# Attention of the last two batches run four groups ahead, and seven products for eight in the last four groups of an attention and mixer kernel

## Chip, core and metric

One NeuronCore of a Trainium2 chip. The metric is the device time of one execution in microseconds (us), the median of several runs. All data are float32.

## What is computed

For 8 batches of 576 tokens, 8 heads of width 64: attention inside chunks of 64 tokens, then a mixer over tokens of rank 32 and a two-layer network over channels (512 to 2048 to 512).

```python
scores = scale * np.matmul(q_c, k_c.transpose(0, 1, 2, 4, 3))   # chunks of 64
attn = softmax(scores); out = np.matmul(attn, v_c)
x = out, heads side by side                                     # 8 x 576 x 512
xt = x.transpose(0, 2, 1)
h = xt @ U @ V                                                  # rank 32, over tokens
u = x + h.transpose(0, 2, 1)
ch = np.maximum(u @ w_ch1, 0.0) @ w_ch2                         # 512 -> 2048 -> 512
return u + ch
```

## The kernel before

**Tiles.** The batches are taken in four pairs (0 to 3). A pair is nine tiles of 128 tokens, and three tiles make a group of 384 tokens, written (pair, group): (0,0) to (3,2), twelve in all. 1_4 is tile 4 of pair 1.

**The channel network.** The 2048 hidden channels are 16 blocks f of 128. For a group and a block, `hidden` (L815) makes h: 12 matmuls of 128x128 by 128x384, each float32 product being three products of a high and a low part. ScalarE takes the high part of its ReLU (L824, hh), VectorE the low part (L829, hl), and `project_out` (L842) adds three times three matmuls of 128x512 into o, one PSUM bank per tile. The loop computes h of block f first and then the o of block f-1, so that hh and hl of a block have the o before and the h after to get done. At the end of a group `finish` (L854) adds o to x and the result is stored (L860).

**The attention of a tile** is steps of one letter in a list per group: n loads q, k, v (L453, L471), t turns q and k (VectorE, L497), s is the scores (L541), maximum, subtraction and exponential, followed at once by the write of the exponentials to DRAM (L493, es) and their fetch back in another layout (L432); q turns them (L497, eT); the next s begins with the products by v (L589, av) of the tile before, the sums (L601) and the scaling to x (L608). p makes the rank-32 product y of a batch (L693 to L730), l adds the mixed part (L748) to x, which is then u (L754), and writes u to DRAM (L488), f fetches it back (L432), u turns it (L497) and splits it (L782, L787). h copies a piece of q or k of a later pair from DRAM to DRAM (L421), waiting for a hidden block.

**Order.** Pair 0's first two groups are issued by a planner (`order`) from the costs and ranks of `Op`s. From (0,2) to (3,0) the loop over f goes through the lists FIRST, LATER and LAST: 64 slots per group (four to a block), the steps spread evenly over the first 58. While a group is computed, the attention of the tiles one to two groups later runs. Within that stretch the engines' orders are those of the tile scheduler, which starts from this order. SP issues nearly all DMAs, in one queue.

**The last two groups,** (3,1) and (3,2), are computed together by `last_groups`, again by the planner. Blocks f = 0 to 3 are as elsewhere. For the six pairs of blocks k = 2 to 7, the 2x2 split (channels in halves, two blocks, two groups) makes h with seven products p (L1162, six matmuls each) in place of eight; sums of u (ra to re, t) are formed once, sums of the weights (sr, s, L1119 to L1137) per k, and VectorE adds up the products (L1183). Free room: weight slots already used up (`wslot`), and eight pieces of the attention's buffers.

Of the kernel before, what the change touches and what calls it, by code (L numbers as in the profile page):

```python
# [23 lines left out]
def kernel(  # L24
# [27 lines left out]
    PLAIN = 2  # L52
    SOFT = (2, 4)
# [447 lines left out]
    def attention_ops(pr, t, *after):  # L501
# [176 lines left out]
        late = [[*soft], [te, ce]] if own else [[*soft, te], [ce]]  # L678
        return [[lq, lk, lv], *turned, *late, [av, sm, x0, x1]]

    ybank = {}
    q_last, tqs, lvs = {}, {}, {}
# [54 lines left out]

    def mix_ops(pr, t, x, ys, after=None, first=None):
        n = f"{pr}_{t}"
        st = {}  # L740
        g, j = divmod(t, GT)

# [19 lines left out]
        def put_u():  # L762
            st["kept"] = put(x_of[pr, t], "us_" + n, by_channel=True)

        def fetch_u():
            tag = {7: "e", 8: "eT"}.get(t, "us") if pr == NPAIR - 1 else "us"
            st["us"] = fetch(st["kept"], slot(tag, F32, "us_" + n, (P, P // SQ, P)))

        def square_u():
            tag = "qk" if pr == NPAIR - 1 and g == 2 else "uT"  # L770
            uT = st["t"] = slot(tag, F32, "uT_" + n)
            square(
                uT.rearrange("p (c j a) -> p a c j", c=NCC, j=SQ), st["us"].rearrange("p a (c i) -> p a c i", i=SQ)
            )

# [8 lines left out]
        def low():  # L784
            uh, ul = ut_of[pr, g]
            js = slice(j * P, (j + 1) * P)
            nc.vector.tensor_sub(ul[:, :, js], st["t"].rearrange("p (c t) -> p c t", c=NCC), uh[:, :, js])  # L787

# [45 lines left out]
    def project_out(pr, g, f, hs, first, final, j):  # L834
        hh, hl = hs
        t = g * GT + j
        if first:
            acc[g, j] = bank(f"o_{pr}_{t}")
        js = slice(j * P, (j + 1) * P)
        prods = [(hh, 0), (hh, 1), (hl, 0)]  # L840
        for i, (h, z) in enumerate(prods):
            nc.tensor.matmul(  # L842
                acc[g, j],
                lhsT=h[:, js],
                rhs=w2[f][:, z],
                start=(first and i == 0),
                stop=(final and i == 2),
            )
        return acc[g, j]
# [140 lines left out]
    def last_groups(mixing, flush):  # L990
        pr = NPAIR - 1
        CC = NCC // 2
# [4 lines left out]
        ROOM.update({"bank": 5, "w": 0, "piece": 8, "c": 3, "h": 1, "x": 0, "ut": 1})  # L997

        def piece(name, tags=itertools.chain(["qk", "qk", "qk", "vn", "vn", "us", "e", "eT"])):
            tag = next(tags)  # L1000
            t = slot(tag, F32R, name, (P, 2, HP, D1) if tag == "vn" else (P, 512))
            t = t.rearrange("p a b c -> p (a b c)") if tag == "vn" else t
            return t[:, 0:GN]

        rest = ["y", "y", "uT", "x", "x", "x"]
        held = {}

        def temp(key, name):
            tag = held[key] = rest.pop(0)
            return work.tile([P, DM], F32, tag=tag, name=name, bufs={"x": NX, "y": 2, "uT": 1}[tag])[:, 0:GN]  # L1010

        def drop(key):
            rest.append(held.pop(key))
# [8 lines left out]
        u_last = []  # L1022
        for t in range(2 * GT, NT):
            _, hi, lo = mixing[t][2]
            his = Op("ACT", 0.59, hi.run, his, take="ut" if t == 2 * GT else "")
            u_last.append(Op("DVE", 0.69, lo.run, his))


        before, plain_done = {}, {}
        d = {1: prev, 2: None}  # L1030
        chain = None
        for f in range(2 * PLAIN):
            for g in (1, 2):
                rank[0] = 10
                a, e, _, _ = chain = block_ops(pr, g, f, f == 0, False, u_last if g == 2 else [], chain)
                if g == 2:
                    e.free = [*e.free, "w"]
                    e.after.append(plain_done[f])
                else:
                    plain_done[f] = e  # L1040
                before[g, f] = a
                d[g] = e
        rank[0] = 0
        for o in ops:
            if o.eng == "PE" and o.rank[0] == 10 and o.name == "hidden":
                o.rank = 11, o.rank[1]

        uh = {g: (lambda g=g: ut_of[pr, g][0]) for g in (1, 2)}
        ul = {g: (lambda g=g: ut_of[pr, g][1]) for g in (1, 2)}
        st = {}  # L1050
        one, two = slice(0, CC), slice(CC, NCC)


        def scratch():
            for n in (2, 3):
                st[n] = [[piece(f"t{n}{z}{c}") for c in range(CC)] for z in range(2)]

        def scratch4():
            t4 = wslot((2, CC, GN), F32R, "t4")
            st[4] = [[t4[:, z, c] for c in range(CC)] for z in range(2)]  # L1060

        def whole(name, g, k):
            st[name] = temp(name, f"r{name}{k}")
            nc.vector.tensor_add(st[name], uh[g]()[:, k].bitcast(F32), ul[g]()[:, k].bitcast(F32))

        def less(out, x, y, fresh=None, over=None):
            if fresh is not None:
                st[out] = temp(out, f"r{out}{fresh}")
            nc.vector.tensor_sub(st[out], st[x], st[y])
            if over is not None:  # L1070
                drop(over)

        def high_of(n, c, x):
            nc.scalar.copy(b_of[n]()[0][c], st[x])

        def low_of(n, c, x):
            nc.vector.tensor_sub(b_of[n]()[1][c], st[x], b_of[n]()[0][c])
            drop(x)
# [3 lines left out]
        z = Op("DVE", 0.01, scratch, *u_last, take="piece " * 8)  # L1082
        for c in range(CC):
# [16 lines left out]
            if c == 0:  # L1100
                z = Op("DVE", 0.01, scratch4, z, take="w")
# [8 lines left out]
        begun_s = [None]  # L1110

        def s_ops(k):
# [3 lines left out]
            def begin():  # L1116
                w["r"] = wslot((8, CC, P), F32, f"sr_{k}")
                for i, f in enumerate((a, b)):
                    nc.vector.tensor_add(  # L1119
                        w["r"][:, 2 * i : 2 * i + 2].rearrange("p a c n -> p (a c) n"),  # L1120
                        w1[f][:, 0].bitcast(F32),
                        w1[f][:, 1].bitcast(F32),
                    )

            def sums():
                r, o = w["r"][:, 0:4], w["r"][:, 4:8]
                nc.vector.tensor_add(o[:, 0], r[:, 2], r[:, 3])
                nc.vector.tensor_sub(o[:, 1], o[:, 0], r[:, 0])
                nc.vector.tensor_sub(o[:, 2], r[:, 0], r[:, 2])
                nc.vector.tensor_sub(o[:, 3], r[:, 1], o[:, 1])  # L1130

            def high():
                w["s"] = wslot((2, 4, CC, P), F32R, f"s_{k}")
                nc.scalar.copy(w["s"][:, 0], w["r"][:, 4:8])

            def low():
                nc.vector.tensor_sub(w["s"][:, 1], w["r"][:, 4:8], w["s"][:, 0])  # L1137

            o = Op("DVE", 1.4, begin, begun_s[-1], take="w")
            o = Op("DVE", 1.7, sums, o)  # L1140
            o = Op("ACT", 1.05, high, o, take="w")
            o = Op("DVE", 1.22, low, o, free="w")
            begun_s.append(o)
            return w, o

        quarter = lambda f, half: (lambda: [[w1[f][:, z, c] for c in range(half * CC, half * CC + CC)] for z in range(2)])
        b_of = {
            "11": lambda: [[u[1]()[:, c] for c in range(CC)] for u in (uh, ul)],
            "21": lambda: [[u[1]()[:, c] for c in range(CC, NCC)] for u in (uh, ul)],
# [226 lines left out]
```

## Time and profile before

| | us |
|---|---|
| median of 3 runs | 928.87 (928.59 to 929.07) |
| profiled execution | 925.92 |
| its span (first to last instruction) | 923.8 |
| TensorE (PE) busy | 907.5 (98%) |
| VectorE (DVE) busy | 511.3 (55%) |
| ScalarE (ACT) busy | 225.4 (24%) |
| mean busy share of 16 DMA engines on q1 | 45.8% |

2.1 us of the profiled execution lie outside its span. PE's busy time includes the pipelined end of each matmul, so that a matmul of 384 columns has a record of 337 ns although one starts every 174 ns; times of stretches are therefore taken from start to start. PEld is PE's weight load, SPq the queue of SP, which issues DMAs. `[0.63 <-DVE hl L829]` behind a row is the idle time before it and what ended it.

### The profile page before, as it was taken

The page shows a single profiled execution, that of the slowest core. Times are in us where ns is not written, and L with a number is a line of the kernel's source. Part 1 is how long each engine was busy: PE and PEld are TensorE (multiplying, and loading weights), DVE is VectorE, ACT ScalarE, POOL GpSimd, SP SyncE. Part 2 cuts the span into 40 slices and gives each one's busy share as a digit, 9 for nine tenths or more (in the row PEclk, how much of TensorE's full clock was granted, in tenths as well). Part 3 has the DMA queues.
Part 4 walks back from the last instruction along what each step waited for, and adds up shares of the span by engine and source line. Part 5 has one row for each costly group of instructions (what it writes and reads, how often), then busy time and mean ns, then how long its engine had stood idle before and what let it go on. Part 6 is the DMA issues. An engine that isn't in the chain of part 4 may idle for free.

```text
span 923.8 us, 16154 instructions
## 1 busy us (share of the span) xinstructions
PE 907.5 (98%) x6594; PEld 797.0 (86%) x6594; DVE 511.3 (55%) x988; ACT 225.4 (24%) x399; POOL 9.7 (1%) x51
## 2 busy tenths in 40 slices
PE   8899999999999999999999999999999999999998
PEld 5569898888898888888898888998889888899886
DVE  4899994274546435544435635553443654678534
ACT  6545441121222111121211211111121121232211
POOL 2000000000000000000000000000000000000000
PEclk9999999999999999999999999999999999999999
DMA  9894477766537525644544624572241515000001
GB/s 185 190 332 138 138 155 110 119 162 147 127 73 179 117 52 138 130 118 91 126 78 105 137 64 109 129 145 71 69 92 34 149 47 113 37 1 1 0 1 69
DMA packets 278713, 98.79 MB, mean 107 GB/s; under 512 B 228464, under 2 KB 264944, under 8 KB 278640
## 3 DMA queue, kind: packets, MB, share of 16 engines
q1 hardware_dynamic: 278384, 97.24, 45.8%
q8 instruction: 52, 0.85, 0.4%
q0 software_dynamic: 256, 0.52, 0.3%
q14 instruction: 21, 0.17, 0.1%
HBM read 73.84 MB, written 37.75 MB: 121 GB/s over the span
## 4 chain that ended last, share of the span: by engine, by line
PE 85%; DVE 6%; DMA 4%; SPq 3%; ACT 2%; issue 1%; ACTq 0%; DVEq 0%
PE o L842 39%; PE h L815 34%; PE p L1162 5%; PE av L589 2%; PE sc L541 2%; DMA wraw<-in_moe_w_ch_dram 2%; SPq L471 1%; PE ps_fill L154 1%; PE y L704 1%; PE y L705 1%; PE u L748 1%; DMA us<-us_3d 1%; DVE w L385 1%; DVE wroom L113 1%; DVE hl L829 1%
## 5 line engine op out<-in xcount | busy, mean ns | idle before, releaser
L815 PE MATMUL h<-uth,w 128*128 128x384 f32 x1344 | 365.0, 337 | 0.8 <-DVE hl L829 0.5
L842 PE MATMUL o<-w,hh 128*128 128x512 f32 x1152 | 347.5, 394 | 0.0
L815 PEld LDWEIGHTS h<-uth,w 128*128 128x128 f32 x1344 | 245.2, 188 | 8.6 <-issue 1.5
L842 PEld LDWEIGHTS o<-w,hh 128*128 128x128 f32 x1152 | 213.7, 188 | 37.4 <-issue 0.5
L815 PE MATMUL h<-utl,w 128*128 128x384 f32 x672 | 226.2, 337 | 0.3 <-DVE utl L787 0.2
L842 PE MATMUL o<-w,hl 128*128 128x512 f32 x576 | 214.1, 395 | 1.0 <-DVE hl L829 1.0
L824 ACT ACTIVATE hh<-h 128x384 fp32r<-128x384 f32 x168 | 82.3, 490 | 367.1 <-PE h L815 366.9
L829 DVE SCALAR_TENSOR_TENSOR hl<-h,hh 128x384 fp32r<-128x384 f32 x168 | 91.9, 548 | 125.5 <-ACT hh L824 125.4
L815 PEld LDWEIGHTS h<-utl,w 128*128 128x128 f32 x672 | 126.1, 188 | 6.4 <-DVE utl L787 1.0
L842 PEld LDWEIGHTS o<-w,hl 128*128 128x128 f32 x576 | 107.5, 188 | 25.3 <-DVE hl L829 1.8
L497 DVE STREAM_TRANSPOSE uT<-us 128x512 f32<-128x512 f32 x27 | 29.6, 1097 | 43.9 <-PE h L815 19.4
L497 DVE STREAM_TRANSPOSE eT<-es 128x512 f32<-128x512 f32 x27 | 29.2, 1081 | 41.3 <-DMA es<-es_7d 8.9
L497 DVE STREAM_TRANSPOSE qT<-qn 128x512 f32<-128x512 f32 x27 | 19.2, 709 | 53.4 <-PE h L815 50.3
L570 ACT ACTIVATE ex<-ex 128x512 f32<-128x512 f32 x36 | 22.8, 634 | 65.4 <-DVE ex L562 61.0
L555 DVE TENSOR_REDUCE mx<-sc 128x4 f32<-128x256 f32 x72 | 28.0, 414 | 14.7 <-PE sc L541 14.7
L693 ACT CAST xh<-x 128x512 fp32r<-128x512 f32 x30 | 18.6, 619 | 66.7 <-DVE x L608 45.4
L754 DVE TENSOR_TENSOR x<-u,x 128x512 f32<-128x512 f32 x36 | 24.4, 686 | 16.8 <-PE u L748 16.6
L782 ACT CAST uth<-uT 128x512 fp32r<-128x512 f32 x27 | 16.5, 620 | 50.3 <-DVE uT L497 50.3
L608 DVE TENSOR_TENSOR x<-av,sm 128x256 f32<-128x256 f32 x72 | 27.2, 417 | 0.9
L697 DVE TENSOR_TENSOR xl<-x,xh 128x512 fp32r<-128x512 f32 x30 | 20.6, 686 | 8.8 <-ACT xh L693 8.0
L589 PEld LDWEIGHTS av<-vn,eT 64*64 64x64 f32 x864 | 15.6, 133 | 10.4 <-issue 10.4
L854 DVE TENSOR_TENSOR x<-o,x 128x512 f32<-128x512 f32 x36 | 23.3, 678 | 1.7 <-PE o L842 1.7
(127 smaller groups left out, 672.0 us busy)
## 6 DMA issues: line engine op xcount, KB each, us to landing
wraw<-in_moe_w_ch_dram SPq DMA_DIRECT2D x32, 512.0 KB
out_dram<-x SPq DMA_DIRECT2D x36, 256.0 KB
halfq<-in_q_dram SPq DMA_DIRECT2D x24, 288.0 KB
halfk<-in_k_dram SPq DMA_DIRECT2D x24, 288.0 KB
qn<-halfq SPq DMA_DIRECT2D x27, 256.0 KB
kn<-halfk SPq DMA_DIRECT2D x27, 256.0 KB
vn<-in_v_dram SPq DMA_DIRECT2D x108, 64.0 KB
qkv<-in_q_dram SPq DMA_DIRECT2D x8, 256.0 KB
```

Source lines behind the costliest of these rows:

```text
L497: turned = nc.vector.transpose(dst, src)
L555: nc.vector.reduce_max(mx, st["sc"][e], axis=AX.X)
L570: nc.scalar.activation(exf, exf, AF.Exp, scale=SCALE)
L589: nc.tensor.matmul(ps[e][cs, hp * D1 : (hp + 1) * D1], lhsT=st["eT_"][rows, hp, cs], rhs=vn[rows, c, hp, :], start=True, stop=True,)
L608: nc.vector.tensor_mul(by_head[:, heads(pr, t, e), :], st["av"][e][:, :, 0:D], st["sm"][:, e].unsqueeze(2).broadcast_to([P, HP, D]),)
L754: nc.vector.tensor_add(x, st["u"], x)
L815: o = nc.tensor.matmul(ps[:, :GN], lhsT=w[:, z, cc], rhs=u[:, cc, :], start=(n == 0), stop=(n == 3 * NCC - 1))
L824: nc.scalar.activation(hh, ps[:, :GN], AF.Relu)
L829: nc.vector.scalar_tensor_tensor(hl, ps[:, :GN], 0.0, hh, op0=ALU.max, op1=ALU.subtract)
L842: nc.tensor.matmul(acc[g, j], lhsT=h[:, js], rhs=w2[f][:, z], start=(first and i == 0), stop=(final and i == 2),)
L854: nc.vector.tensor_add(x, ps, x)
L1162: nc.tensor.matmul(ps[:, :GN], lhsT=w[x][c], rhs=u[y][c], start=(n == 1), stop=(n == 3 * CC))
```

## The change

- **Steps at slots of their own.** The lists are replaced by one table, STEPS, for (0,2) to (2,1), in which each step has its slot. The steps of (0,2) stand where they stood. From (1,0) on the attention goes faster: six, four, five, four and two tiles begin in the five groups, where it had been three, four and two in each three groups. It is over in (2,1), two groups earlier than before. The exponentials' write (e) and fetch (E) are steps of their own, 2 to 4 slots apart, and c (the split of x) is taken out of p.
- **u kept in DRAM.** From tile 1_3 on, u is also written whole to DRAM (24 writes of 256 KB), which frees the x buffer, and fetched back before the group ends: twelve by the step r, twelve in the last groups.
- **Four last groups.** `last_groups` calls `two_groups` twice: (2,2) with (3,0), then (3,1) with (3,2). Its four plain blocks now run first for the one group, then for the other. Two weights' sums are formed in six buffers of 512 words a partition taken from the nine x buffers, in four pieces instead of one, and the sums of u in the attention's pieces and in the room of `ust` and `vst`. The u of (3,0) is turned at the start of the first call, that of (3,1) and (3,2) fetched behind the second product of its last k.

```diff
+    SPILLED = 1, 3
-            kept = put(flat(), "es_" + n)
-            st["es"] = fetch(kept, slot("e", F32, "es_" + n, (P, P // SQ, P)))
+        def put_e():
+            st["kept"] = put(flat(), "es_" + n)
+        def get_e():
+            st["es"] = fetch(st["kept"], slot("e", F32, "es_" + n, (P, P // SQ, P)))
...
+    def bring(pr, t, x):
+        nc.sync.dma_start(x, whole_u[pr, t])
+        x_of[pr, t] = x
...
             st["kept"] = put(x_of[pr, t], "us_" + n, by_channel=True)
+            if (pr, t) >= SPILLED:
+                whole_u[pr, t] = dram.tile([P, DM], F32, name=f"u_{n}d")
+                nc.sync.dma_start(whole_u[pr, t], x_of[pr, t])
...
+        first = u_ready(mixing, 3, 0, prev)
+        tail = two_groups(0, (2, 2), (3, 0), [prev], [], first, prev)
+        first = u_ready(mixing, 3, 1, tail[1])
+        second = u_ready(mixing, 3, 2, tail[1])
+        two_groups(1, (3, 1), (3, 2), [tail[0]], first, second, tail[0])
...
-        for f in range(2 * PLAIN):
-            for g in (1, 2):
+        for g in (1, 2):
+            for f in range(2 * PLAIN):
...
+            us = ust.rearrange("p a j r -> p (a j r)")
+            st[4] = [[us[:, 0:GN], us[:, GN : 2 * GN]], [us[:, 2 * GN : 3 * GN], vst[:, 0:GN]]]
...
-                nc.scalar.copy(w["s"][:, 0], w["r"][:, 4:8])
-                nc.vector.tensor_sub(w["s"][:, 1], w["r"][:, 4:8], w["s"][:, 0])
+            for i, over in ((1, None), (2, None), (0, 1), (3, 0)):
+                h = Op("ACT", 0.41, lambda i=i: high(i), o, take="s")
+                ready[i] = Op("DVE", 0.42, lambda i=i, over=over: low(i, over), h, free="" if over is None else "s")
+            begun_s[:] = [ready[3]]
...
+                        back[g, j] = Op("SP", 0.5, home, *formed.values(), take="s", dma=1.0, n=128, lat=2.0)
...
+            begun_s.append(u4)
+        return hl, p2
...
-    LAST = "t6 . q5 s6 . l3 n7 . f3 . t7 q6 . s7 u3 . n8 . p0 t8 . q7 s8 . ...
+        ((1, 1), "s22@1 n23@1 h@1 f16@4 e22@4 l18@4 E22@8 h@8 u16@10 t23@10 q22@12 s23@14 n24@15 h@15 f17@16 ...
...
-                while done < len(steps) and done * (NF * 4 - TAIL) < len(steps) * slots:
+                while steps and int(steps[0][1]) <= slots:
```

The slots of the scores in STEPS: (0,2) 5, 14, 25, 35; (1,0) 5, 15, 25, 36, 50; (1,1) 1, 14, 29, 43, 57; (1,2) 7, 22, 36, 50; (2,0) 1, 15, 29, 43, 57; (2,1) 8, 22, and the last av at 38. In the lists before: FIRST 5, 14, 25, 35; LATER (1,0) 4, 14, 26; (1,1) 6, 20, 35, 49; (1,2) 12, 26.

## Rows read from the trace of the kernel before

**Rows 1.** Page, chain that ended last: shares by engine.
```profile
PE 85%; DVE 6%; DMA 4%; SPq 3%; ACT 2%; issue 1%; ACTq 0%; DVEq 0%
```
**Rows 2.** Windows: length, busy PE, PEld, DVE, ACT, POOL, PEclk, DMA share, GB/s.
```profile
272.30:792.00 519.70, 517.77 (x3816) 460.80 (x3815) 246.54 (x492) 98.70 (x187) 2.26 (x20) 1.00 0.45 102
...
347.30:417.20 69.90, 69.90 (x556) 62.70 (x555) 34.57 (x71) 12.16 (x23) 0.34 (x3) 1.00 0.56 128
491.90:567.70 75.80, 74.99 (x576) 66.38 (x575) 36.44 (x75) 14.57 (x28) 0.45 (x4) 1.00 0.48 107
...
712.60:792.00 79.40, 78.36 (x588) 68.86 (x587) 43.00 (x84) 16.32 (x31) 0.23 (x2) 1.00 0.37 90
...
823.50:919.80 96.30, 96.27 (x478) 85.90 (x476) 55.17 (x102) 20.54 (x35) 0.00 (x0) 1.00 0.02 8
```
**Rows 3.** Waits of PE's weight loads, 272 to 800 us: total, times, longest.
```profile
PEld av L589 <- issue: 8.4, 24, 0.4
PEld u L748 <- DVE ys L730: 1.1, 1, 1.1
...
PEld h L815 <- DVE hl L829: 0.8, 2, 0.6
```
**Rows 4.** Chain in order of time: plain blocks, the end; start, us, what.
```profile
796.72 4.12 PE o L842 x18
800.85 4.16 PE h L815 x24
805.01 4.12 PE o L842 x18
...
904.65 15.13 PE o L842 x66
```
**Rows 5.** Groups by line on PE, 823.5 to 919.8 us: busy us, mean ns.
```profile
L842 PE MATMUL o<-w,hh 128*128 128x512 f32 x150 | 46.7, 393 | 0.0
L842 PE MATMUL o<-w,hl 128*128 128x512 f32 x76 | 29.7, 391 | 0.0
```
**Rows 6.** Groups by line on DVE, 823.5 to 904.5 us: weights' sums.
```profile
L1137 DVE TENSOR_TENSOR s<-sr,s 128x1024 fp32r<-128x1024 f32 x5 | 6.1, 1223 | 1.1 <-ACT s L1134 1.0
...
L1128 DVE TENSOR_TENSOR sr<-sr 128x256 f32<-128x256 f32 x4 | 1.7, 425 | 0.1
```
**Rows 7.** Timeline of PE: end of the last k's second product, next o.
```profile
894.50 0.34 PE L1162 MATMUL p<-uth,w 128*128 128x384 f32 x1
894.67 0.62 PE L842 MATMUL o<-w,hh 128*128 128x512 f32 x2
```
**Rows 8.** Timeline of PE: scores of one tile, then its av.
```profile
218.41 0.65 PE L541 MATMUL sc<-kT,qT 64*64 64x64 f32 x32
230.76 0.70 PE L589 MATMUL av<-vn,eT 64*64 64x65 f32 x32
```
**Rows 9.** Timeline of SP: that tile's exponentials out and back.
```profile
223.87 0.54 SPq L493 DMA_DIRECT2D es_3d<-ex  x1
226.59 0.34 SPq L432 DMA_DIRECT2D es<-es_3d  x1
```
**Rows 10.** Timeline of DVE: the turn of that tile's exponentials.
```profile
229.30 1.10 DVE L497 STREAM_TRANSPOSE eT<-es 128x512 f32<-128x512 f32 x1 [3.14 <-DMA es<-es_3d]
```
**Rows 11.** Timeline of SP: the same out and back at 160 us.
```profile
160.66 0.37 SPq L493 DMA_DIRECT2D es_0d<-ex  x1
163.59 0.33 SPq L432 DMA_DIRECT2D es<-es_0d  x1
```
**Rows 12.** Timeline of DVE: its turn.
```profile
166.44 1.10 DVE L497 STREAM_TRANSPOSE eT<-es 128x512 f32<-128x512 f32 x1 [0.52 <-DMA es<-es_0d]
```
**Rows 13.** Window from 160 us, columns as in rows 2.
```profile
160.00:180.00 20.00, 20.00 (x104) 18.40 (x103) 4.00 (x6) 3.09 (x6) 0.00 (x0) 1.00 0.69 121
```
**Rows 14.** Window of the end: six tiles are stored, nothing else moves.
```profile
904.60:923.80 19.20, 15.17 (x67) 12.10 (x65) 7.83 (x13) 3.16 (x6) 0.00 (x0) 1.00 0.22 83
```
**Rows 15.** SP's issue of a store: ns min/median/max, first and last start.
```profile
L860 SPq DMA_DIRECT2D out_dram<-x x36: 332/398/1446, 186.8 to 920.5; - x36
```

More of the change, by code (lines that the diff above doesn't have):

```diff
@@ L996, in last_groups @@
         ROOM.clear()
[L997 to L1013, printed above, removed]
+        ROOM.update({"bank": 5, "piece": 5, "c": 3, "s": 6, "h": 1, "ut": 1})
         prev = None
@@ new lines, in last_groups, with u_ready @@
+        tail = two_groups(0, (2, 2), (3, 0), [prev], [], first, prev)
+        first = u_ready(mixing, 3, 1, tail[1])
+        second = u_ready(mixing, 3, 2, tail[1])
+        two_groups(1, (3, 1), (3, 2), [tail[0]], first, second, tail[0])
+    def u_ready(mixing, pr, g, after):
+        his = None
+        los = []
+        for j in range(GT):
+            _, (fe,), (tr, hi, lo) = mixing[pr, g * GT + j]
+            o = None
+            if g:
+                o = Op("SP", 0.6, fe.run, after, take="piece", dma=1.3, n=512, lat=2.0)
+            o = Op("DVE", 1.1, tr.run, o, take="piece", free="piece")
+            his = Op("ACT", 0.59, hi.run, o, his, take="" if j else "ut")
+            los.append(Op("DVE", 0.69, lo.run, his, free="piece"))
+        return los
@@ L1050, in last_groups @@
+        ul = {g: (lambda g=g: ut_of[G[g]][1]) for g in (1, 2)}
         st = {}
-        one, two = slice(0, CC), slice(CC, NCC)
         def scratch():
[L1055 to L1060, printed above, removed]
+            for m in (2, 3):
+                st[m] = [
+                    [unit(PIECES, ("t", n, m, z, c), F32R, f"t{n}{m}{z}{c}")[:, 0:GN] for c in range(CC)]
+                    for z in range(2)
+                ]
+            us = ust.rearrange("p a j r -> p (a j r)")
+            st[4] = [[us[:, 0:GN], us[:, GN : 2 * GN]], [us[:, 2 * GN : 3 * GN], vst[:, 0:GN]]]
@@ new lines, in high, with low @@
+            def high(i):
+                s = unit(FORMS, (n, "s", i, k), F32R, f"s{n}{i}_{k}").rearrange("p (z c m) -> p z c m", z=2, m=P)
+                w["s", i] = s
+                nc.scalar.copy(s[:, 0], w[i])
+            def low(i, over):
+                nc.vector.tensor_sub(w["s", i][:, 1], w[i], w["s", i][:, 0])
+                if over is not None:
+                    drop(FORMS, (n, "r", over, k))
+            o = Op("DVE", 1.4, whole_w, *begun_s, take="s s")
+            o = Op("DVE", 1.7, sums, o)
@@ L1313, in go @@
                 mixing["p"] = project_ops(at, e, [None] * NT)[0]
[L1314 removed]
+            do(mixing["p"][k][:2])
+        elif kind == "p":
+            do(mixing["p"][i % 5][2:])
         elif kind == "l":
[L1316 to L1324 removed]
+            mixing[at, i] = mix_ops(at, i, None, [None, None])
+            do(mixing[at, i][0])
+        elif kind == "r":
+            bring(at, i, work.tile([P, DM], F32, tag="x", name=f"x_{at}_{i}b", bufs=NX))
+        else:
+            do(mixing[at, i]["lfu".index(kind)])
@@ L1337 @@
             pend = (pr, g, f, hs)
-        assert done == len(steps)
+        assert not steps
     manual = tc.manual_schedule(engines=None)
```

292 lines of the change are left out of this document (149 added, 143 removed), and 9 rows, old and new, of tables (LATER, STEPS).

## Prediction

> **What bounds the kernel now.** I read the chain of work first: TensorE (PE) holds 85% of it, DMA 4%, SP's queue 3% [rows 1]. Then the windows by stage, to see where PE is idle: 1.93 us in the seven groups from (1,0) to (3,0), of which 0.81 in (2,0) and 1.04 in (3,0) and none in (1,1), at a full clock everywhere; VectorE (DVE) is busy for 47% of those seven groups, DMA for 0.45 [rows 2]. Then PE's waits in the middle: the largest is 8.4 us, 24 times 0.36 us ahead of av with no releaser, which comes with each switch to 64x64 blocks and goes with the work; real waits are 1.1 us for y and 0.8 for hl [rows 3]. So this is a kernel bound by the number of matmuls: little can be won by hiding, and much lost by a delay that is long enough to reach PE.
>
> **What the seven products are worth.** Two plain o blocks start 8.29 us apart with an h between each (796.72 to 805.01), so one (group, f) costs 4.145 us: 2.08 for twelve matmuls of h (0.174 each) and 2.06 for nine of o (0.229 each) [rows 4]. The stretch of the last two groups with seven products lasts 96.30 us [rows 2]. Of its 226 o matmuls 216 belong to its six k, and nine, 9 x 0.229 = 2.06 us, to the plain block ahead [rows 5]; that leaves 94.24 us for work that takes 24 x 4.145 = 99.48 us in plain blocks. One application saves **5.2 us**. By count it would be six times one product of six matmuls, 6 x 6 x 0.174 = 6.3 us; I take the measured 5.2, since switches and waits for VectorE are in it, and keep 6.3 as the far end.
>
> The change applies it once more, to (2,2) and (3,0): **-5.2 us**, all of it on PE, which is the path.
>
> **What the second application adds beside PE.** The low part of the weights' sums, one subtraction of 1.22 us per k, becomes four of 256 elements, which by the nearest row take 0.43 each [rows 6]: 1.7 for 1.22, so +0.5 us of VectorE per k, 6 us over twelve k. VectorE is busy 55.2 of 96.3 us there and ScalarE 20.5 [rows 2], so PE's products cover it: 0. The next k's sums now wait for the last add that frees the sums' buffers; behind that wait stand 4 to 5 us of sums on VectorE, and PE has two products and up to twelve o triples (12 x 0.69) to do meanwhile: 0, and if that cover is gone at most some 1 us per k, 6 us for the first application (kept in the upper end).
>
> **The two seams.** The second application's first plain block needs the u of (3,1), fetched behind the last k's second product. In the present kernel that product ends at 894.7 us [rows 7] and the last o at 919.8 [rows 4], a cover of 25 us. The chain is a fetch (0.33 issue, 2.7 to land, as for es [rows 9, 10]), three turns of 1.10 us [rows 10] and a cast and a subtraction behind the last: about 7.6 us. It lies beside the o: 0. The seam from the loop into the first call has 16.6 us of plain blocks of (2,2), 4 x 4.145, to turn the three tiles of (3,0): 0.
>
> **What is moved.** Nothing is added to PE: av, scores, y and u are the same instructions, in fewer groups. From the start of (1,0), 272.3, to the last o at 919.8 there are 647.5 us; the last four groups will take two times the 127.8 us of the present last two (792.0 to 919.8) [rows 2], so with 5.2 saved the five groups (1,0) to (2,1) get 647.5 - 5.2 - 255.6, about 387 us, for what now stands in 519.7. Everything off PE gets denser by a third. VectorE does 246.5 us there [rows 2], of which 2 x 16 x 0.55 belong to hl of the two groups that leave; the rest is 59% of 387: covered.
>
> *DMA.* The share of 0.45 [rows 2] is 234 us of the 16 engines. 24 writes and 12 of the 24 reads of x join here, the other reads in the last groups, where DMA moves next to nothing. The window with six stores of just this shape and nothing else shows 0.22 of 19.2 us, 4.2 us, 0.7 per transfer [rows 14]; 36 make 25 us. The share becomes (234 + 25) / 387, about 0.67. None of it is on PE's path as long as round trips fit.
>
> The Trainium skill (DMA: Bandwidth & Descriptors, Bandwidth, with the fit of its section on one DMA's anatomy) puts it worse for this change: batch to 1 MiB, since each DMA has some 2.0 us fixed beside its bytes. By that fit a 256 KB piece takes an estimated 2.6 us, 36 take 94, and were that occupancy, not latency, the share would be 0.85. The trace's 0.7 us decides against that reading.
>
> *Round trips.* Scores to av of one tile took 12.35 us at 218 us: 5.5 to the write's issue, 2.7 to the fetch, 2.7 to the turn, 1.1 of turn and a little [rows 8 to 10]. The new table spaces scores 14 or 15 slots apart in most places, of 1.09 us each (69.9 / 64 in (1,1) [rows 2]), 15.3 us for 14; in (0,2) the slots are unchanged; only (1,0) has three spaces of 10 or 11, as LATER and FIRST had. At a share of 0.69 the same legs took 2.9 and 2.9 us [rows 11 to 13], so the legs do not grow at the share that is coming. (1,1), with 14 to 15 slots, is the stretch without idle PE [rows 2].
>
> *SP.* Each of the 48 moves takes 0.40 us of issue as a store does [rows 15], 19 us in all. Behind a write of u that waits for VectorE's add stand the loads of the next tile and the next fetch; the write of exponentials no longer waits in front of other issues, since it has a slot after the exponential. I take 0 net; bounds below.
>
> *Waits of PE.* Of the 1.93 us of idle time in rows 2 the 1.04 us of (3,0) goes with that stretch, and the 0.81 of (2,0), which had three tiles 10 to 12 slots apart, may go. New waits come in (1,0), with six tiles. Ends: all 1.9 us gained, or, since (2,0) lost 0.8 us on three tiles, 0.27 on each of 21 tiles begun from (1,0) on, 5.7 us lost and 1.9 won. I take **-1.0 us**, nearest to (1,1), whose spacing the table has.
>
> **Sum.** 925.92 - 5.2 - 1.0 = 919.7 us for a profiled execution like the one shown. The median is 2.95 us above that execution: **922.7 us**.
>
> **Rivals.**
> 1. *Round trips come late* (slower). DMA and SP are a third denser; if fetches of exponentials land 3.5 us later than now, 12.35 becomes 15.9 and passes the 15.3 us of 14 slots. VectorE then stands at the turn, hl behind it, and PE at av: 0.6 us on each of some 20 tiles, 12 us. 922.7 + 12 = 934.7 us. It decides from 3 us of delay. For it: VectorE already waits 3.1 us at one turn [rows 10]. Against it: the legs at a share of 0.69 [rows 11 to 13].
> 2. *A seam lies bare.* If the 7.6 us chain isn't started early, PE ends the first application and waits, 922.7 + 7.6 = 930.3 us, about no change. Against it: 25 us of cover.
> 3. *The attention doesn't get done in time.* Five tiles' u are added in the last four slots of (2,1), with 25 writes; x buffers are full at several places, and a tile's x waits until a write lands. If that costs what one stretch with waits shows, 1.0 us, in each of five groups, the gain is gone: 927.7 us.
> 4. *All waits go* and the product is worth 6.3 us: 925.92 - 6.3 - 1.9 + 2.95 = 920.7 us.
>
> **Numbers.** Chances: the forecast 0.62 (with 920.5 to 925.5 around it), rival 4 0.09, rival 3 0.07, rival 2 0.07, rival 1 0.15. A measurement of this kernel tells a change from 0.2%, 1.9 us, on, that is below 927.0 or above 930.7. Faster takes the forecast, rival 4 and about half of rival 3: 0.74. Same takes the other half and most of rival 2: 0.09. Slower takes rival 1 and the rest: 0.17. The range goes from 919.8, just beyond rival 4, to 930.0, which takes in rival 3, the upper ends of the unknown waits and nearly rival 2, and leaves out rival 1.
>
> **What would show it.** Right: a second stretch of some 94 us with 252 p and 216 o ahead of (3,1); the span some 6 us shorter; (1,0) with under 1.5 us of idle PE; share of DMA about 0.65 in (1,0) to (2,1) with legs of es still near 2.7 us. Wrong: VectorE's waits at eT for es above 4 us, a PE gap of several us at the start of (3,0) or (3,1), or waits of p for the weights' sums at each k. The sign falls if the five groups (1,0) to (2,1) take over 393 us.

## The result and the profile after

The changed kernel takes **938.38 us** (median of 4 runs, 936.43 to 942.03), the kernel before beside it 928.73: a ratio of 1.0114 [1.0079, 1.0149], slower by 1.1% where faster by 0.7% was forecast. The profiled execution took 938.73 us, its span 937.0.

First the chain of work that ended last, by engine, as in [rows 1]:

```profile
PE 80%; DVE 7%; SPq 6%; DMA 4%; issue 2%; ACT 1%; DVEq 0%; POOL 0%; ACTq 0%; POOLq 0%
```

PE lost five points and SP's queue gained three. Then the windows by group, columns as in [rows 2]: (1,0), (1,1), (1,2), (2,0), (2,1), the last four groups together, and in them the new stretch of seven products:

```profile
273.20:359.50 86.30, 79.94 (x673) 70.66 (x672) 46.77 (x98) 15.87 (x29) 0.57 (x5) 0.96 0.69 153
359.50:440.10 80.60, 77.79 (x669) 69.30 (x668) 40.78 (x90) 16.17 (x30) 0.56 (x5) 0.98 0.70 156
440.10:522.90 82.80, 78.96 (x609) 68.87 (x608) 44.18 (x89) 15.56 (x30) 0.45 (x4) 0.98 0.67 155
522.90:599.50 76.60, 76.60 (x671) 67.93 (x670) 41.71 (x91) 15.86 (x30) 0.56 (x5) 1.00 0.52 140
599.50:678.30 78.80, 78.03 (x526) 68.53 (x525) 38.78 (x74) 14.92 (x28) 0.11 (x1) 1.00 0.39 103
678.30:933.00 254.70, 254.12 (x1273) 229.14 (x1272) 173.06 (x348) 65.43 (x149) 0.00 (x0) 1.00 0.13 39
711.60:806.00 94.40, 94.40 (x472) 84.88 (x471) 67.95 (x136) 24.44 (x55) 0.00 (x0) 1.00 0.12 42
```

The last four groups took 254.7 us where 255.6 were forecast: the seven products came as promised. The first five took 405.1 where 387 were forecast. All that was lost, 18 us, lies in (1,0), (1,1) and (1,2); (2,0) and (2,1), in the same form, stand at 76.6 and 78.8.

Two things make up the loss. The first is idle time of PE; its waits from 273 to 678 us (total, times, longest):

```profile
PE av L596 <- issue: 9.3, 3, 5.0
PE h L853 <- DVE hl L867: 1.7, 2, 1.3
PE h L853 <- DVE x L615: 1.6, 2, 1.3
PE o L880 <- DVE hl L867: 0.8, 1, 0.8
PE y L714 <- DVE xl L706: 0.4, 1, 0.4
```

13.8 us in all, 9.3 of them three waits at av. The second is the clock. Windows of the largest gap with what follows, and of the three stretches at half:

```profile
293.00:303.70 10.70, 5.67 (x76) 4.92 (x76) 4.25 (x11) 1.25 (x2) 0.11 (x1) 0.68 0.72 134
296.80:303.60 6.80, 4.90 (x72) 4.62 (x73) 4.25 (x11) 1.25 (x2) 0.11 (x1) 0.50 0.60 124
382.10:385.50 3.40, 3.40 (x11) 3.40 (x12) 2.28 (x7) 0.63 (x1) 0.00 (x0) 0.50 0.71 214
505.00:508.40 3.40, 3.40 (x59) 2.96 (x59) 3.06 (x11) 0.26 (x1) 0.11 (x1) 0.50 0.38 101
```

Each of the three begins in a gap at av or less than 2 us behind one, and PE ran at 1.2 GHz (granted clock 0.50) for 6.8, 3.4 and 3.4 us. Of these 13.6 us 4.9 + 3.4 + 3.4 = 11.7 have work in them, which at 2.4 GHz would have taken half: an estimated 5.9 us. With the gaps that is 19.7, against 18 missing, since the 387 us already held the 1.9 us of idle time of the kernel before.

Now the first gap from PE outward. Timeline of PE: the scores of tile 1_6, the last o, and the av of 1_6:

```profile
280.32 0.65 PE L542 MATMUL sc<-kT,qT 64*64 64x64 f32 x32
...
292.82 0.85 PE L880 MATMUL o<-w,hl 128*128 128x512 f32 x3
298.70 1.15 PE L596 MATMUL av<-vn,eT 64*64 64x65 f32 x30 [5.03 <-issue]
```

The profile puts the gap down to nothing ("issue"). VectorE's timeline shows what av waited for, the turn that ends at 298.60:

```profile
297.52 1.08 DVE L498 STREAM_TRANSPOSE eT<-es 128x512 f32<-128x512 f32 x1 [6.80 <-DMA es<-es_6d]
```

ScalarE made the exponentials of 1_6, ready at 284.2, and SP's line shows why they were back so late (timelines of ScalarE and SP):

```profile
283.56 0.63 ACT L571 ACTIVATE ex<-ex 128x512 f32<-128x512 f32 x1 [3.15 <-DVE ex L563]
...
283.99 0.43 SPq L454 DMA_DIRECT2D qn<-halfq  x1
284.53 0.63 SPq L472 DMA_DIRECT2D vn<-in_v_dram  x1
285.25 0.55 SPq L454 DMA_DIRECT2D kn<-halfk  x1
285.86 1.92 SPq L472 DMA_DIRECT2D vn<-in_v_dram  x3
287.87 0.55 SPq L494 DMA_DIRECT2D es_6d<-ex  x1
288.47 0.78 SPq L422 DMA_DIRECT2D halfk<-in_k_dram  x1
289.35 2.61 SPq L422 DMA_DIRECT2D halfq<-in_q_dram  x1
292.06 2.86 SPq L433 DMA_DIRECT2D es<-es_6d  x1
```

The write goes out 3.7 us behind the exponential's end, with loads of the next tile ahead of it. The fetch goes out 4.2 us behind the write, with two copies of halves between them, and its own issue, 0.34 us in [rows 9], is held for 2.86. From ready to the turn it took 13.3 us. PE had 13.35 us of work between the scores and the av (280.32 to 293.67); the way took 18.4. In the kernel before the same tile had had 14.9 us and no gap (timelines of PE, ScalarE, SP and VectorE):

```profile
277.35 0.69 PE L541 MATMUL sc<-kT,qT 64*64 64x64 f32 x32
281.29 0.63 ACT L570 ACTIVATE ex<-ex 128x512 f32<-128x512 f32 x1 [0.44 <-DVE ex L562]
284.29 0.45 SPq L493 DMA_DIRECT2D es_6d<-ex  x1
284.80 1.70 SPq L488 DMA_DIRECT2D us_3d<-x  x3
286.82 0.33 SPq L432 DMA_DIRECT2D es<-es_6d  x1
289.52 1.09 DVE L497 STREAM_TRANSPOSE eT<-es 128x512 f32<-128x512 f32 x1 [3.00 <-DMA es<-es_6d]
292.26 0.70 PE L589 MATMUL av<-vn,eT 64*64 64x65 f32 x32
```

Its turn began 7.6 us after the exponential's end. The 5.7 us between 13.3 and 7.6 are, leg by leg: 1.3 for the later write (3.7 for 2.4), 1.7 for the later fetch (4.2 for 2.5), 2.5 for the fetch's held issue (2.86 for 0.33), and 0.2 from the issue's end to the turn (2.6 for 2.4). The fetch must wait for the write to land in either kernel, so that only 1.7 of its 4.2 us are new.

The gaps at 378 (tile 2_2) and 501 us (tile 3_0) are of the same kind, 12.5 and 10.8 us from the exponential to the turn. At 2_2 the write goes out 5.0 us behind the exponential's end, and a store, four writes of us and one of u stand between write and fetch; at 3_0 a read of u stands there, held for 3.50 us behind a copy.

### The profile page after: what moved, and what is told of

It is laid out like the page before. It is cut to its first block, busy times and chain, and to the rows that moved or that the text cites. A ratio compares the mean times of both kernels' runs of the same rounds, so it can differ in the third digit from the quotient of the medians.

```text
span 937.0 us, 16467 instructions
## 1 busy us (share of the span) xinstructions
PE 907.8 (97%) x6558; PEld 796.5 (85%) x6558; DVE 570.5 (61%) x1132; ACT 241.4 (26%) x455; POOL 9.7 (1%) x51
## 4 chain that ended last, share of the span: by engine, by line
PE 80%; DVE 7%; SPq 6%; DMA 4%; issue 2%; ACT 1%; DVEq 0%; POOL 0%; ACTq 0%; POOLq 0%
PE o L880 37%; PE h L853 28%; PE p L1198 9%; PE av L596 2%; SPq L472 2%; SPq L460 1%; PE sc L542 1%; DVE hl L867 1%; SPq L489 1%; DVE wroom L114 1%; DVE wroom L117 1%; PE y L714 1%; PE y L713 1%; DMA es<-es_8d 1%; DVE w L386 1%
## 5 line engine op out<-in xcount | busy, mean ns | idle before, releaser
L853 PE MATMUL h<-uth,w 128*128 128x384 f32 x1152 | 315.6, 339 | 3.2 <-DVE hl L867 1.7
L853 PEld LDWEIGHTS h<-uth,w 128*128 128x128 f32 x1152 | 212.0, 189 | 10.8 <-issue 3.0
L880 PE MATMUL o<-w,hl 128*128 128x512 f32 x576 | 218.5, 397 | 2.0 <-DVE hl L867 2.0
L853 PE MATMUL h<-utl,w 128*128 128x384 f32 x576 | 195.0, 338 | 0.1
L862 ACT ACTIVATE hh<-h 128x384 fp32r<-128x384 f32 x144 | 70.5, 490 | 293.4 <-PE h L853 293.3
L867 DVE SCALAR_TENSOR_TENSOR hl<-h,hh 128x384 fp32r<-128x384 f32 x144 | 78.7, 547 | 97.8 <-ACT hh L862 97.4
L853 PEld LDWEIGHTS h<-utl,w 128*128 128x128 f32 x576 | 108.9, 189 | 5.4 <-DVE utl L823 0.5
L596 PE MATMUL av<-vn,eT 64*64 64x65 f32 x864 | 21.8, 230 | 9.7 <-issue 9.7
L1198 PE MATMUL p<-t,s 128*128 128x384 f32 x144 | 29.2, 337 | 0.1
## 6 DMA issues: line engine op xcount, KB each, us to landing
halfq<-in_q_dram SPq DMA_DIRECT2D x24, 288.0 KB
halfk<-in_k_dram SPq DMA_DIRECT2D x24, 288.0 KB
```

Source lines behind the costliest of these rows:

```text
L596: nc.tensor.matmul(ps[e][cs, hp * D1 : (hp + 1) * D1], lhsT=st["eT_"][rows, hp, cs], rhs=vn[rows, c, hp, :], start=True, stop=True,)
L853: o = nc.tensor.matmul(ps[:, :GN], lhsT=w[:, z, cc], rhs=u[:, cc, :], start=(n == 0), stop=(n == 3 * NCC - 1))
L862: nc.scalar.activation(hh, ps[:, :GN], AF.Relu)
L867: nc.vector.scalar_tensor_tensor(hl, ps[:, :GN], 0.0, hh, op0=ALU.max, op1=ALU.subtract)
L880: nc.tensor.matmul(acc[pr, g, j], lhsT=h[:, js], rhs=w2[f][:, z], start=(first and i == 0), stop=(final and i == 2),)
L1198: nc.tensor.matmul(ps[:, :GN], lhsT=w[x][c], rhs=u[y][c], start=(m == 1), stop=(m == 3 * CC))
```

## The experiments

Results are ratios to the kernel before, run on the same chip, with the 95% interval; "the five groups" are (1,0) to (2,1).

The theories at the start. **Q**: SP's one line delays the round trip of the exponentials, above all where an issue stands right behind a copy of halves (2304 packets of 128 bytes): 11 such issues from 272 to 600 us took 2.86 us in the mean, the others 0.60. (In the kernel before only two issues behind 272 us were held so, both copies themselves.) **D**: the 16 DMA engines are too full. **U**: the added writes and reads of whole u. Later **R** joined: the scores at the start of (1,0), 10 to 11 slots apart, leave too little room.

**1. Copies of halves on GpSimd's queue** (h_pool).

```diff
-        moved = nc.sync.dma_start(
+        moved = (nc.gpsimd if b >= 4 else nc.sync).dma_start(
```

> Changed kernel, but the copies of halves of batches 4 to 7 (26 of them from (1,0) to (1,2)) are issued by GpSimd's queue instead of SP's. Theory Q (SP's queue is held for 2.4 to 2.9 us by whatever is issued right behind a copy of halves, and fetches of exponentials and of u stand there): the holds go from SP, PE's idle time in (1,0) to (1,2) falls from 13 us to under 4, no stretch at half clock, 919 to 925 us. Theory D (the 16 DMA engines are too full for the round trips): the same packets move, 936 to 941 us. Theory U (the whole writes and reads of u are too much): 936 to 941 us.

1.0254 [1.0232, 1.0275]. Worse. On GpSimd the copies share a line with the ones in v's tiles, which wait for an av (waits on GpSimd, 200 to 680 us):

```profile
POOL vn L447 <- PE av L596: 135.6, 15, 19.1
```

Such a wait delays a copy only where one stands behind it, and how much of the loss comes from there was not separated. VectorE waited 8.0 us for a load of q at 289 us, and the write of the exponentials of 1_6 went out 8.5 us behind their end, although no copy stood in SP's line. The run decides nothing on Q or D.

**2. Copies in pairs, right behind a fetch of exponentials** (h_behind). The h steps move in the table, and each copy is ordered behind the last fetch.

```diff
+            nosync = mybir.DependencyInfo(mybir.DependencyClass.NoSync, mybir.DependencyReason.DATA)
+            tc.add_manual_dep(moved.ins, fetched[-1].ins.name, nosync, reason="behind this fetch")
...
-n17@5 h@6 e16@8 E16@10 t17@10 h@10
+n17@5 e16@8 E16@10 h@10 h@10 t17@10
```

> Changed kernel, but from (1,0) to (1,2) the copies of halves stand in pairs directly behind a fetch of exponentials E, with an order dependency on that fetch, never between a write e and its fetch. Theory Q: the 5 us wait of av at 293 us and the half clock behind it go; the second copy and the load behind a pair are still held, so some waits stay: 924 to 932 us. Theory D: 936 to 941 us. Theory U: 936 to 941 us.

1.0204 [1.0179, 1.0229]. At 1_6 the round trip took 8.0 us, nearly as short as before the change, and the gap of 5.0 us at av fell to 0.4: there the copies were the cause. But the hold had moved to the next fetch in line, that of u:

```profile
317.99 3.71 SPq L422 DMA_DIRECT2D halfq<-in_q_dram  x2
321.81 2.89 SPq L438 DMA_DIRECT2D us<-us_3d  x1
```

VectorE waited 5.5 us for it, and PE 7.1 for an x behind it on VectorE. A second gap of 7.1 us, at 473, is behind another late fetch of u (waits of PE, 272 to 680 us):

```profile
PE h L858 <- DVE hl L872: 7.5, 2, 7.1
PE h L858 <- DVE x L620: 7.1, 1, 7.1
```

What stood right behind a copy was held; in a line this full it was again something urgent.

**3. No whole writes and reads of u** (no_u). Its 24 writes and 24 reads are left out and x is set to zero instead, so that the output lacks u of those tiles in the last sum.

```diff
-        nc.sync.dma_start(x, whole_u[pr, t])
+        nc.gpsimd.memset(x, 0.0)
...
-                nc.sync.dma_start(whole_u[pr, t], x_of[pr, t])
```

> Changed kernel without the 24 whole writes of u and the 24 fetches back; GpSimd sets the x tile to zero where it was fetched, so the residual of those tiles is missing from the output. Copies of halves as in the changed kernel. Theory Q: the holds behind copies of halves stay, only the places where writes of u stand between e and E (1.5 to 2.6 us at 377 and 500 us) get shorter: 930 to 937 us. Theory D: 25 of 260 us of DMA time go, 932 to 937 us. Theory U: 919 to 925 us.

1.0105 [1.0062, 1.0149], where the changed kernel has 1.0114. U falls as the cause: with 12.6 MB less on the DMA engines and 48 issues less on SP the time stays within the interval, and PE waits 11.6 us at av.

**4. The same moves on GpSimd's queue** (u_pool).

```diff
-                nc.sync.dma_start(whole_u[pr, t], x_of[pr, t])
+                nc.gpsimd.dma_start(whole_u[pr, t], x_of[pr, t])
```

> Changed kernel, but the 24 whole writes of u and the 24 fetches back are issued by GpSimd's queue. Theory Q: copies of halves still hold SP; SP has 24 us of issue less: 931 to 938 us. Theory D: the same bytes move, 936 to 941 us. Theory U: 936 to 941 us if it is the traffic, 920 to 928 us if it is SP's issue time.

1.0146 [1.0114, 1.0177], no gain.

**5. Copies of halves on ScalarE's queue** (h_act).

```diff
-        moved = nc.sync.dma_start(
+        moved = (nc.scalar if b >= 4 else nc.sync).dma_start(
```

> The copies of halves of the last two batches (2,304 small packets each) are issued on ScalarE's own DMA queue instead of SyncE's; nothing else differs, GpSimd's queue is left as it was, and the bytes on the 16 DMA engines are the same. Theory Q (SyncE's one in-order queue: a fetch of e or a load issued right behind a copy of halves is held 2.4 to 2.9 us, where others take 0.57): no issue on SyncE is held over 2 us in 272 to 530 us, the legs from e's write to its exponentials come back to some 3 us each, the TensorE gaps of 5.0, 2.5 and 1.8 us at 294, 378 and 501 go, the clock stays at full, and the time is 919 to 927. The price is on ScalarE: some 26 issues, of up to 2.9 us each, of which it has room for some. Theory D (the 16 DMA engines are too full in this stretch, whichever queue issues): the legs stay long and the time is 935 to 941. If the cost of issuing only moves to ScalarE and it falls behind with its evictions of PSUM: 930 to 945 with TensorE waiting for ScalarE.

1.0168 [1.0151, 1.0185]: a miss. No copy holds an issue on SP any more, and yet the write at 1_6 is later still (8.4 us behind its exponential):

```profile
286.07 8.24 SPq L472 DMA_DIRECT2D vn<-in_v_dram  x4
294.41 0.77 SPq L494 DMA_DIRECT2D es_6d<-ex  x1
```

SP's waits say what one of the four loads of v ahead of it stood for:

```profile
SPq L472 <- DMA halfk<-in_k_dram: 5.4, 1, 5.4
```

It waits for a copy of k that it shares no data with: the program's DMAs on SP and ScalarE take eight completion counters (semaphores) in turn, and a DMA waits until the one eight places ahead has landed. In the trace the same eight semaphores come round over both engines' issues, and this load has the copy's. No such wait stands among SP's waits in the changed kernel, 272 to 680 us. So the run took away the held issues and put the landing of a copy in their place; it doesn't tell what the holds alone cost. What it shows is that the write can be late without them, through whatever stands ahead of it in the line.

**6. Write and fetch directly behind the scores** (e_in_s), as in the kernel before, in the table of the five groups.

```diff
-s16@5 n17@5 h@6 e16@8 E16@10 t17@10
+S16@5 n17@5 h@6 t17@10
```

> e's write and its fetch are put back directly behind their sums (one place in line, as in the kernel before) in the five groups; the copies of halves, the four-groups-ahead plan, the writes of u and the seven-product groups stay. Theory Q: the write of e is issued up to 3 us sooner, but copies of halves still come between write and fetch where the scheduler puts them, so the held fetches remain in part: 928 to 936, with gaps on TensorE of half the 13.7 us. Theory D: 935 to 941. If the places in line of e were needed to keep VectorE's line from standing (the change's own reason): slower than the changed kernel, 940 or more.

1.0130 [1.0107, 1.0153], no change. The tile scheduler puts the write where its own estimate of times says, and that is behind the loads in either table (the write of 1_6 goes out at 288.0 us, for 287.9 in the changed kernel). The places for e and E in the change did nothing for the round trip.

**7. Both** (h_act_e). The edits of 5 and 6.

> Both edits: copies of halves on ScalarE's queue, and e's write and fetch directly behind the sums. Theory Q: both delays on SyncE gone, 918 to 925. Theory D: 935 to 941. If it equals the run with ScalarE's queue alone within 1 us, the place of e's write costs nothing once the held issues are gone.

1.0129 [1.0113, 1.0144], no better than the changed kernel; PE still stands 6.0 us at the av of 1_6.

**8. Loads of v on GpSimd's queue** (v_pool).

```diff
-                queue = nc.gpsimd if plain(pr, t) and t in SOFT else nc.sync
+                queue = nc.gpsimd if not plain(pr, t) or t in SOFT else nc.sync
```

> The loads of v of the three pairs that are not plain ones (some 108 issues of 0.6 us, on SyncE in the changed kernel) go to GpSimd's queue; the copies of halves stay on SyncE. Theory Q in its weak form (too much issuing on SyncE in all, 241 us behind 272): SyncE is some 65 us emptier over the whole kernel, but the holds of 2.9 us behind a copy of halves stay, so 929 to 936. Theory Q in its strong form (only the holds behind the copies count): no change, 935 to 940. Theory D: 935 to 941. If GpSimd's queue stands for a zeroing of tiles that waits for TensorE, v comes late: 940 or more.

1.0065 [1.0037, 1.0093]: some 0.5 points back, with bytes and copies unchanged, from an emptier line alone; the interval still touches the changed kernel's. The gap at av at 294 us is still 4.6.

**9. The exponentials' round trip on ScalarE's queue** (e_act2). Now the urgent thing itself leaves the line.

```diff
-            st["kept"] = put(flat(), "es_" + n)
+            st["kept"] = put(flat(), "es_" + n, queue=nc.scalar if (pr, t) >= (1, 6) else nc.sync)
...
-            st["es"] = fetch(st["kept"], slot("e", F32, "es_" + n, (P, P // SQ, P)))
+            st["es"] = fetch(
+                st["kept"], slot("e", F32, "es_" + n, (P, P // SQ, P)), nc.scalar if (pr, t) >= (1, 6) else nc.sync
+            )
```

> From tile 1_6 on the write of the exponentials and its fetch are issued on ScalarE's queue, where the exponential itself is made, so that neither stands behind loads, writes of u or copies of halves in SyncE's line; the bytes and the order of everything else stay. Theory Q (the round trip of the exponentials is late because of its place in SyncE's one line): write within 0.5 us of the exponential's end, fetch 3 us later, turn 2.8 us after that, at tile 1_6 some 7 us sooner than the 13.3 us of the changed kernel, where TensorE then needn't wait; the TensorE gaps at av (5.0, 2.5, 1.8 us) and the half-clock stretches behind them go, 921 to 928. Theory D (the 16 DMA engines are too full): write and fetch themselves take over 4 us each and the time stays at 935 to 941. Theory R (three tiles 10 to 11 slots apart at the start of group (1,0) leave too little room, whatever the queue): the gap at 294 us shrinks by less than half, 931 to 938. If ScalarE stands too long at the fetch for the write to land, hh comes late: gaps of TensorE at o or h, 930 or more.

**0.9978 [0.9966, 0.9990]**: from 1.1% slower to 0.2% faster than the kernel before. ScalarE's timeline at tile 1_6, whose exponential ends at 284.0:

```profile
285.90 0.42 ACTq L494 DMA_DIRECT2D es_6d<-ex  x1
286.37 0.49 ACT L864 ACTIVATE hh<-h 128x384 fp32r<-128x384 f32 x1 [2.36 <-DMA u_3d<-x]
289.82 0.34 ACTq L433 DMA_DIRECT2D es<-es_6d  x1
```

and VectorE's turn, 3.4 us sooner than in the changed kernel:

```profile
294.10 1.08 DVE L498 STREAM_TRANSPOSE eT<-es 128x512 f32<-128x512 f32 x1 [2.82 <-DMA es<-es_6d]
```

The write still waited 1.9 us for u_3d, whose counter it has, another wait of the kind of run 5. So the turn came half as much sooner as the 7 us expected: write to fetch took 3.9 us, fetch to turn 4.3. At the three tiles with gaps, 1_6, 2_2 and 3_0, the way from exponential to turn is 10.1, 9.4 and 7.4 us, for 13.3, 12.5 and 10.8. The windows of (1,0) and (1,1):

```profile
273.00:356.20 83.20, 78.25 (x674) 68.76 (x673) 47.32 (x99) 15.74 (x29) 0.56 (x5) 1.00 0.74 160
356.20:432.80 76.60, 76.51 (x668) 67.83 (x667) 39.74 (x87) 15.28 (x28) 0.56 (x5) 1.00 0.73 163
```

The clock stays full, and the DMA engines are busier than in the slow kernel, 0.74 and 0.73 for 0.69 and 0.70. **D falls** as the cause of the loss. (The kernel before says so too: its round trip of 1_6 took 7.6 us in a window at a share of 0.90.)

```profile
281.90:289.50 7.60, 7.60 (x41) 6.95 (x40) 2.19 (x4) 1.00 (x3) 0.00 (x0) 1.00 0.90 205
```

Of the 13.5 us by which the profiled span is shorter than the changed kernel's, 8.0 are idle time of PE (5.8 us left in the five groups, for 13.8), and an estimated 5.9 are the clock, which here stayed full behind gaps of 1.8 and 1.7 us. That part is partly luck: in run 10 a gap of 1.9 us at the same place was followed by 3.4 us at half clock.

Another reading would be that ScalarE's queue carries the same bytes faster. It doesn't: from the end of an issue to the last update of its counter a write of exponentials took 3.10 us and a fetch 2.95 in the mean of the 19 tiles up to 600 us, for 2.72 and 2.45 on SP in the changed kernel. What got shorter is the wait ahead of the issue: 0.3 us from the exponential's end to the write, for 1.7, and no fetch's issue took over 0.4 us.

The Trainium skill (DMA: Bandwidth & Descriptors, Issuing engines are not separate DMA queues) says that starting DMAs on several engines "will only save the time on the sequencer it takes to initiate the DMA, which is usually small relative to the DMA itself". By that rule this run would gain next to nothing; its ratio is 1.36 points lower, because what it saves is not the 0.4 us of an issue but the place in a line.

**10. The same, with v on GpSimd's queue** (e_act2_v). The edits of 8 and 9.

> As the run with the exponentials' round trip on ScalarE's queue, and the loads of v of pairs 1 to 3 on GpSimd's queue as well (3.5 us gained alone). Theory Q: both add up, 917 to 924, below the kernel before. Theory D: 933 to 941. Theory R: 927 to 935.

0.9973 [0.9958, 0.9988]: the loads of v add nothing to speak of once the round trip is out of their way.

**11. More room at the start of (1,0)** (early). The scores of 1_6 go to slot 51 of (0,2), of 1_7 to 6, 1_8 to 19, 2_0 to 35; the steps around them go along. No queue changes.

```diff
-... u11@52 f12@54 u12@57"),
+... t16@46 f11@49 q15@49 l12@50 S16@51 u11@52 n17@52 f12@54 u12@57"),
-t16@1 q15@3 l13@4 s16@5 n17@5 ... q16@13 s17@15 ... s18@25 ... s20@36
+t17@1 q16@3 l13@4 s17@6 n18@6 ... q17@17 ... s18@19 ... s20@35
```

> Only places in the table change: the scores of tile 1_6 go from slot 5 of group (1,0) to slot 51 of group (0,2), those of 1_7 to 6, 1_8 to 19, 2_0 to 35, so that the spaces at the start of (1,0) are 19, 13 and 16 slots instead of 10, 10 and 11; all queues stay as in the changed kernel. Theory R: the 5.0 us gap of TensorE at 294 us and the 6.8 us of half clock behind it go, 8 to 9 us in all, and the later gaps stay: 928 to 932. Theory Q: the delay in SyncE's line is as long as before, but with 2 to 3 slots (2 to 3.5 us) more room it hides in part: 931 to 936. Theory D: 935 to 941.

1.0046 [1.0029, 1.0062], 0.7 points back. (1,0) takes 76.9 us, without a gap and at full clock, though the exponentials of 1_7 still need 11.2 us to their turn: with room the delay is hidden. Part of this is moved: (0,2), which took over the scores of 1_6, is some 3 us longer, 1.6 of them a gap of PE at 267 us. (1,1) and (1,2), where nothing was changed, keep their gaps:

```profile
PE av L596 <- issue: 3.7, 2, 2.2
```

**12. The same with v on GpSimd's queue** (early_v).

> The changed places of the early scores and the loads of v on GpSimd's queue together. Theory R with what the loads gave alone: 925 to 929. Theory Q: 927 to 934. Theory D: 934 to 941.

0.9991 [0.9976, 1.0005], no change to the kernel before, and 0.55 points below run 11: with more room, and the round trip still on SP, the emptier line counts.

**13. The write alone on ScalarE's queue** (e_act).

```diff
-            st["kept"] = put(flat(), "es_" + n)
+            st["kept"] = put(flat(), "es_" + n, queue=nc.scalar if (pr, t) >= (1, 6) else nc.sync)
```

> Only the write of the exponentials goes to ScalarE's queue; the fetch stays on SyncE. If the write's place in SyncE's line is the larger part of the delay (3.7 and 5.0 us behind the exponential's end at tiles 1_6 and 2_2 of the changed kernel, fetches at 4.2 and 4.8 us): 927 to 932, most of the 13 us that both together gave back. If the fetches held behind copies of halves are the larger part: 932 to 937.

1.0040 [1.0024, 1.0056], half of what both gave. (1,2) is mended (76.9 us); in (1,0) the fetch of 1_6 still goes out 5.8 us behind its write, and 4.8 us of gap remain. Write and fetch are both late in the line, each at its own places.

**14. Room and ScalarE's queue together** (early_e). The edits of 9 and 11.

> The earlier scores at the start of group (1,0) and the exponentials' round trip on ScalarE's queue together; loads of v on SyncE. What is left with the queue alone is 5.7 us of TensorE gaps, 4.9 of them in group (1,0). If room in the table and place in the queue are two halves of one delay, they go: 920 to 924, under the kernel before by 0.4% or more. If the ScalarE queue alone had already taken all that can be had: 924 to 927.

**0.9964 [0.9951, 0.9977]**, 923.63 us. All waits of PE from 272 to 680 us:

```profile
PE o L882 <- DVE hl L869: 0.8, 1, 0.8
PE av L598 <- issue: 0.5, 1, 0.5
```

Ahead of this window, in (0,2), PE stands 1.5 us at 264.5, where the earlier scores now are.

**15. All three** (early_ev): 8, 9 and 11.

> All three: earlier scores, the exponentials' round trip on ScalarE's queue, the loads of v on GpSimd's. 919 to 923.5 if the loads add as little as they did beside the ScalarE queue (0.5 us); this is the version expected to beat both kernels, near the 922.7 of the prediction.

**0.9949 [0.9932, 0.9966]**, 922.92 us, below both kernels. Of the ratio 1.0114 of the changed kernel the queue alone takes 1.36 points, the room alone 0.68, both together (run 14) 1.50, not the sum 2.04, which fits one delay mended from its two ends. The interval overlaps that of run 14; whether the loads of v add anything is not decided. A gap of 1.9 us at 266.7, in (0,2), is left, with 3.4 us at half clock behind it.

**16. The kernel before with the round trip on ScalarE's queue** (before_e).

```diff
-            kept = put(flat(), "es_" + n)
-            st["es"] = fetch(kept, slot("e", F32, "es_" + n, (P, P // SQ, P)))
+            queue = nc.scalar if (pr, t) >= (1, 6) else nc.sync
+            kept = put(flat(), "es_" + n, queue=queue)
+            st["es"] = fetch(kept, slot("e", F32, "es_" + n, (P, P // SQ, P)), queue)
```

> The kernel before, with the exponentials' write and fetch from tile 1_6 on issued on ScalarE's queue, nothing else. If the queue matters only where the attention runs dense (the theory: the kernel before has 1.9 us of idle TensorE in all), the time stays within 0.2% of the kernel before, 926 to 930. If ScalarE's queue is a gain of its own, whatever the plan: 915 to 925, and then what the changed kernel won back by it says nothing on its plan.

0.9991 [0.9981, 1.0001], no change. The queue is no gain of its own; it gives back what the denser attention had lost. Here too the transfers themselves landed later on ScalarE's queue, 3.03 and 2.60 us for 2.39 and 2.34 (means from 272 to 678 us).

## Why the prediction was wrong

- **Seven products, -5.2 us: right.** The new stretch of 94.4 us lies where it should, with PE busy throughout and VectorE busy for 68.0 of it; the four last groups took 254.7 us for 255.6. (Its sum places 225 of the 226 o matmuls; the one left is 0.23 us.)
- **Seams and added VectorE work, 0: right.** PE stands 0.6 us in those 254.7. The added work was larger than the sum had it, 3 us for each application: VectorE is busy for 68.0 us in the new stretch and 58.8 from 839 to 933 us, for 55.2 in [rows 2]. It stayed beside PE all the same.
- **The work of the five groups, 387 us: right.** Run 9 took 392.2 in them, 386.4 without its 5.8 us of idle PE.
- **DMA share about 0.67: too high, and beside the point.** It was 0.60 over 272.3 to 678.3 us, and up to 0.70 by group; run 9 has 0.74 and is no slower than the kernel before. By the fit named in the prediction, which its section gives for DMAs issued from GpSimd, it would have been 0.85.
- **"SP: I take 0 net": the step that failed.** It added up issues, 19 us (the 48 moves took 28), and not places in a line. The question was what stands ahead of the write and the fetch of each tile when they become ready: at 1_6 loads, then copies with a hold behind them, 5.5 us more than in the kernel before. Three such waits, 9.3 us, and the clock behind them made most of the 18 us that the five groups took beyond their 387. [Rows 11 to 13], taken as proof that "the legs do not grow at the share that is coming", were legs in a stretch where nothing stood between write and fetch. They showed the DMA engines' part, and were read as the whole round trip. That part grew little: from issue's end to landing 2.72 us for a write and 2.45 for a fetch in the mean, for 2.39 and 2.34 in the kernel before.
- **"Only (1,0) has three spaces of 10 or 11, as LATER and FIRST had": named and passed over.** The room of a 10-slot space, 13.35 us from scores to av, was never set against the 12.35 us of [rows 8 to 10]: 1 us to spare. That such spaces had cost 0.8 us at most in the kernel before was taken as enough, but there tile 1_6 had 14.9 us, and its write went out 2.4 us behind its exponential, not 3.7.
- **The clock was in no term.** A gap was priced at its length. The three at av, 9.3 us, were followed by 13.6 us at half clock, an estimated 5.9 more.
- **Rival 1 came true in mechanism and place:** VectorE at the turn, hl behind it, PE at av, 934.7 for 938.4. It decided "from 3 us of delay"; 1_6 had 5.7 (13.3 for 7.6). Its price came near by chance: it had 0.6 us at each of some 20 tiles, and what came was three long gaps and the clock. The 0.15 it got was too little, because the evidence against it was the misread rows.
- **The forecast, 0.7% under the kernel before,** is nearly what the plan takes once the delay is out: run 9, with the table unchanged, is 0.2% under it (925.19 us), run 15, with the table and two queues changed, 0.5% (922.92). What was missed is mainly one kind of wait; the worth of the parts was right.

## What to carry to other kernels

When work is packed more densely, price each queue by position: for every round trip that a busy engine waits for, list what stands ahead of its issues in the same line, and compare the whole way with the room in the plan, not with an average busy share. A round trip that was short of room did best here on another line, that of the engine that makes its data; moving one kind of bulk out of its way mostly changed which bulk was ahead (runs 1, 2, 4 and 5 gained nothing, run 8 some 0.5 points). And price a gap of the matmul engine with the half clock that can follow it.

## What the runs showed of the hardware

- An issue right behind the issue of a copy of 2304 packets is held: 2.35 to 3.50 us, 2.86 in the mean of 11 in the changed kernel, for 0.60 otherwise. The copy's own issue takes 0.78.
- A high share of busy DMA engines alone did not make a round trip of 256 KB each way long: in the kernel before it took 7.6 us from the exponentials to the turn at a share of 0.90. Issued on ScalarE's queue, with the rest on SP's, the transfers landed 0.3 to 0.6 us later in the mean, in either kernel (runs 9 and 16); why was not tried.
- Short gaps can cost clock: in the changed kernel PE stood 2.47 us at 378.0 and 0.34 at 381.6, and 1.82 at 501.3 and 0.40 at 504.2, and each pair was followed by 3.4 us at 1.2 GHz. In run 9 PE stood 1.79 us at 293.5 and 1.66 and 1.50 at 320 to 325, and the clock stayed at 2.4 GHz. In run 11 it stayed behind 2.18 and 0.34 us and fell behind 1.48 and 0.40; in runs 10 and 15 it fell behind 1.85 and 1.92 us alone. What decides between these was not tried.
